# FFN2 of batch 7 by seven block products, a tile of batch 4 as the last piece, and another order of the work

## The chip, the cores and the metric

The kernel runs on one core of a Trainium2 chip. The metric is the time of one execution on the device, in microseconds (us); lower is better. Before the change the median of three runs is 163.83 us (163.65 to 164.19).

The engines, by the names that the profile uses: PE (TensorE) multiplies matrices and writes PSUM, which has eight banks of 128 x 512 fp32; PEld is its loading of weights; DVE (VectorE) and ACT (ScalarE) read PSUM and do elementwise work; POOL (GpSimd) does elementwise work on SBUF and issues the casting loads; SP (SyncE) issues the stores. Each engine takes its instructions in the order in which they were issued to it and waits for the inputs of the next one. 16 DMA engines move the data.

## What is computed

```python
def _attn_ref(q, k, v, phi):                    # 8 batches, 8 heads, 576 rows, D = 64; M = 32
    a = phi - np.max(phi, axis=2, keepdims=True)
    a = np.exp(a)
    a = a / (np.sum(a, axis=2, keepdims=True) + 1e-09)
    k_m = np.einsum('bhsm,bhsd->bhmd', a, k)
    v_m = np.einsum('bhsm,bhsd->bhmd', a, v)
    scores = np.matmul(q, k_m.transpose(0, 1, 3, 2)) / np.sqrt(q.shape[-1])
    scores = scores - np.max(scores, axis=-1, keepdims=True)
    attn = np.exp(scores)
    attn = attn / (np.sum(attn, axis=-1, keepdims=True) + 1e-09)
    return np.matmul(attn, v_m)

def _moe_ref(x, w1, w2, w3, w_out):             # x: 4608 x 512; w1, w2, w3: 512 x 768; w_out: 768 x 512
    h = np.maximum(np.maximum(x @ w1, x @ w2), x @ w3)
    return h @ w_out
```

`x` is the attention's output with the heads side by side. Inputs and output are fp32.

## The kernel before

**What is folded away.** The attention's output of a head is `attn @ v_m`, with only 32 columns in `attn`. So the kernel never forms `x`: for each batch it multiplies `v_m` into the weights (`fold`, line 426) and works on `attn`, whose inner size is 8 heads x 32 = 256. With w1 - w3 and w2 - w3 in place of w1 and w2, the hidden layer is h = max(attn wp_1, attn wp_2, 0) + x w3, and the last part goes straight to the output: out = hT w_out + attn wp3, where wp3 holds v_m, w3 and w_out multiplied together.

**Tiles of rows.** Two batches make a pair with 1152 rows, nine tiles of 128: tiles 0 to 3 of the even batch (rows 0 to 511), tile 4 across both batches (rows 512 to 639), tiles 0 to 3 of the odd batch (rows 640 to 1151).

**The order is written by hand.** The loop at lines 758 to 787 walks a string of words such as `F8@2!` and calls `issue(batch, name, swap)` for each. All engines' instructions come out in that order, and each engine keeps its own share of it. `!` swaps the engine of a step where it has a choice. A second string, `banks` (line 141), gives the PSUM bank of each step that needs one, in the same order; `one_bank` and `two_banks` take the next digit. The names of the steps, with `@b` for the batch:

- L0, L3, L1, L2: loads of phi, q, k, v on POOL's DMA queue (lines 94, 113, 98), 576 KB each. phi and q have two buffers, k and v one for even and one for odd batches.
- r0, r1: pack k and v (L108 on POOL, or L106 on ACT with `!`). E: exponential of phi on ACT (L232).
- B: 72 small matmuls that make k_m and v_m (L250); they need E, r0 and r1. N: normalization on DVE (L270 to L285). K: transposes on PE (L300) and a copy. Q0, Q1: q transposed on DVE (L315). S: scores on PE (L335), then their exponential on ACT (L344).
- a, s, c, m, X: the second normalization, by transpose, sum, reciprocal (DVE), product (POOL, L411) and transpose back (DVE, L419), for two halves 0 and 1.
- D0 to D2: folds of the weights of the hidden layer, D3: fold for wp3 (PE L442, evacuated by ACT or DVE).
- F0 to F11: hidden layer, four matmuls of 288 columns each (L468). An even F ends in a relu on ACT (L173; DVE with `!`, L177), the odd F after it in a maximum on DVE (L481).
- T0 to T4: a plain tile of the output: six matmuls of 512 columns on hT (L658), two on attn (L667; four of half height for T4, L676), a copy by ACT or DVE, a store by SP.

**Seven products.** For the 512 rows of tiles 0 to 3 of a batch, the output can be had from products of blocks half the size: inner size in two halves, output columns in two halves, rows in two groups, seven block products in place of eight, with sums and differences of blocks as operands. Before the change this is done for batches 5 and 6. Its steps:

- U0 to U3 (`combine_w`, line 507): combinations of weight blocks; `U@9` those of w_out, once, 128 x 768 into `tw`; `U@5`, `U@6` those of wp3, 128 x 256. POOL, or DVE with `!`.
- A0 to A3 (`combine_a`, line 552): combinations of blocks of hT, 128 x 768; A4 to A7: of attn, 128 x 256. DVE, or POOL with `!`. A0 and A1 feed one another and then A3; A2 writes over its own block.
- P0 to P6 (`products`, line 565): eight matmuls of 256 columns each (L600). P0, P1 and P2 take a bank each; P3 adds to the bank of P0, P4 to P6 to that of P1. The banks are read into fp32 snapshots (L612 on DVE, L614 on ACT) and added on DVE (L641); two stores of 512 KB follow on SP (L645), the first after P3 and P4, the second after P6.

`combine_w`, `combine_a` and `products` are written for any batch; for batch 7 `sums` (line 521) has buffers of its own, made of those of q, and the output buffers are made of those of phi.

**The last piece.** `ffn2` hands one tile to `ffn2_last` (line 690), which makes it in two column halves of eight matmuls of 256 columns (L699, L707), so that the first half is copied and stored while the second is computed. Before the change this is tile 3 of batch 7.

Of the kernel before, what the change touches and what calls it, by code (L numbers as in the profile page):

```python
# [15 lines left out]
def kernel(  # L16
# [14 lines left out]
    B, H, S, D = q.shape  # L31
# [104 lines left out]
    for i in range(P // M):  # L136
# [4 lines left out]
    banks = iter(  # L141
        "".join(
            """
            00232204420145545045024602460260426042672643424260246024604260462342656204502406
            24062046204267240670462064260246024602064326247420640642064024620462042604605264
            620502645264034063460406064026042640246204203406767676
            """.split()
        )
    )
# [1 line left out]
    def one_bank():  # L151
        return psum[:, int(next(banks))]
# [16 lines left out]
    def evacuate(kind, n, swap, out_, in_, relu=False):  # L169

        if (EVAC[kind][n] == "a") != swap:
            if relu:
                nc.scalar.activation(out=out_, in_=in_, func=AF.Relu)  # L173
            else:
                nc.scalar.copy(out=out_, in_=in_)  # L175
        elif relu:
            nc.vector.tensor_scalar_max(out=out_, in0=in_, scalar1=0.0)  # L177
        else:
            nc.vector.tensor_copy(out=out_, in_=in_)
# [469 lines left out]
    def ffn2(b, t, swap):  # L649


        hT, attn = hts[b // 2], attns[b // 2]
        c0 = S - HP if t == 4 else (b % 2) * (S + HP) + t * P
        if b == B - 1 and t == 3:
            return ffn2_last(b, c0)
        po = one_bank()
        for n, fc in enumerate(fts[b]):
            nc.tensor.matmul(  # L658
                po,
                lhsT=hT[:, fc, c0 : c0 + P],  # L660
                rhs=wo_sb[:, fc, :],
                start=(n == 0),
                stop=False,
            )
        for g in range(NG):
            if t < 4:
                nc.tensor.matmul(  # L667
                    po,
                    lhsT=attn[:, g, c0 : c0 + P],
                    rhs=wp3s[b][:, g, :],  # L670
                    start=False,
                    stop=(g == NG - 1),
                )
            else:
                for u in range(2):
                    nc.tensor.matmul(  # L676
                        po[HP * u : HP * (u + 1)],
                        lhsT=attn[:, g, c0 + HP * u : c0 + HP * (u + 1)],
                        rhs=wp3s[b - 1 + u][:, g, :],
                        start=False,  # L680
                        stop=(g == NG - 1),
                        tile_position=(0, HP * u),
                    )
        ot = opool.tile([P, DM], FP32, name="ot")
        r0 = (b // 2) * 2 * S + c0
        rows = out[r0 : r0 + P, :]
        evacuate("T", t, swap, ot, po)
        nc.sync.dma_start(out=rows, in_=ot)

    def ffn2_last(b, c0):  # L690

        hT, attn = hts[b // 2], attns[b // 2]
        ot = opool.tile([P, DM], FP32, name="ot")
        r0 = (b // 2) * 2 * S + c0
        for i in range(2):
            c = slice(i * DM // 2, (i + 1) * DM // 2)
            po = one_bank()[:, 0 : DM // 2]
            for n, fc in enumerate(fts[b]):
                nc.tensor.matmul(  # L699
                    po,  # L700
                    lhsT=hT[:, fc, c0 : c0 + P],
                    rhs=wo_sb[:, fc, c],
                    start=(n == 0),
                    stop=False,
                )
            for g in range(NG):
                nc.tensor.matmul(  # L707
                    po,
                    lhsT=attn[:, g, c0 : c0 + P],
                    rhs=wp3s[b][:, g, c],  # L710
                    start=False,
                    stop=(g == NG - 1),
                )
            rows = out[r0 : r0 + P, c]
            if i == 0:
                nc.vector.tensor_copy(out=ot[:, c], in_=po)
                nc.sync.dma_start(out=rows, in_=ot[:, c])
            else:
                nc.scalar.copy(out=ot[:, c], in_=po)
                nc.scalar.dma_start(out=rows, in_=ot[:, c])  # L720

    def issue(b, n, swap):
# [22 lines left out]
            "D": lambda: fold(b, i, swap),  # L745
            "F": lambda: ffn1(b, i, swap),
            "T": lambda: ffn2(b, i, swap),
            "U": lambda: combine_w(b, i, swap),
            "A": lambda: combine_a(b, i, not swap),
# [8 lines left out]
    for w in """  # L758
        E@0 H2@0 H0@0 L3@0 Z25@0 B0@0 Y2@0 I@0 N0@0 Z2@0 K0@0! Q0@0 Q1@0 Z9@0 S@0 Z2@0
        M0@0 M1@0 R0@0 R1@0 W0@0 Y3@0 W1@0 W2@0 Z6@0 O1@0 H3@0 O3@0 O2@0 H1@0 X1@0 B1@0  # L760
        X0@0 N1@0 K1@0 O0@0 Y0@0 D1@0! D0@0! D3@0 F8@0 F10@0 F2@0 V0@0 F6@0 F0@0! Y1@0
        D2@0 D4@0 F4@0 L0@1 V1@0 F1@0 E@1 F3@0 L1@1 F5@0 F9@0 F7@0 L3@1 F11@0 B0@1 T3@0
        N0@1 K0@1! L2@1 Q1@1 L2@2 L1@2 Q0@1 L0@2 V2@0 T0@0! L3@2 S@1 T1@0 a0@1 s0@1 c0@1
        m0@1 B1@1 N1@1 a1@1 L1@3 K1@1 s1@1 D0@1 D1@1! D2@1 c1@1 m1@1 X0@1 L3@3 r1@2 X1@1
        T2@0! L2@3 F6@1 F10@1 F7@1 F2@1 F3@1 F4@1 F0@1 r0@2 E@2 F5@1 F1@1 F11@1 L0@3
        L0@4 F8@1 L2@4 F9@1 B@2 D3@1 N@2 Q1@2 T0@1! K@2 T2@1! r0@3 Q0@2 S@2 a0@2 a1@2
        s1@2 c1@2 m1@2 T4@1! D1@2! s0@2 D2@2 c0@2 m0@2 X1@2 D0@2 T3@1 Q0@3 L3@4 X0@2
        Q1@3 T1@1 F0@2 F4@2 F8@2 F6@2 F9@2 E@3 F7@2 F1@2 L1@4 r1@3 F10@2 F2@2 L2@5 B@3
        N@3 D3@2 F3@2 L1@5 F5@2 K@3! U0@9 F11@2 S@3 U1@9 E@4 T3@2 L0@5 T0@2! a1@3 D1@3!
        s1@3 D2@3 a0@3 r1@4 c1@3 L3@5 D0@3 T1@2 m1@3 s0@3 Q0@4 X1@3 c0@3 m0@3 X0@3 T2@2!  # L770
        F4@3! r0@4 F5@3 L2@6 F0@3 D3@3 B@4 F6@3 N@4 F1@3 F8@3 Q1@4 F2@3 F9@3 K@4! F10@3
        r1@5 F7@3 S@4 F11@3 L3@6 D3@4 E@5 r0@5 F3@3 a0@4 U3@9 L0@6 a1@4 T4@3! L1@6 L0@7
        s1@4 D0@4 D1@4! B@5 c1@4 N@5 T1@3 Q1@5 K@5 L1@7 Q0@5 s0@4 c0@4 m0@4 T3@3! S@5
        a0@5 T2@3! s0@5 a1@5 c0@5 X0@4 m1@4 X1@4 D2@4 D0@5 D1@5 m0@5 s1@5 X0@5 T0@3!
        F4@4 c1@5 F2@4 m1@5 r1@6 L2@7 F10@4 r0@6 F3@4 F5@4 F8@4 X1@5 F9@4 F0@4 F11@4
        F6@4 E@6 F10@5! F7@4 L3@7 F0@5 F2@5 A4@5! Q0@6 A5@5! F1@4 F1@5 A7@5! F8@5 F6@5
        F4@5! Q1@6 D3@5 B@6 N@6 r0@7 D2@5 T0@4! F7@5 F5@5 K@6 F3@5 U2@9 F9@5 U0@5! T1@4!
        F11@5 A0@5 A6@5 r1@7! E@7 S@6 T2@4! D1@6! U1@5! D2@6 a0@6 Q1@7 B@7 A1@5! U2@5
        U3@5 N@7 T3@4 s0@6 K@7! Q0@7 a1@6 P1@5 D3@6 s1@6 c1@6 S@7 c0@6 A2@5! m1@6 P2@5
        P4@5 a0@7 s0@7 D3@7 D2@7 m0@6 a1@7 c0@7 D1@7! P0@5! A3@5! U0@6 s1@7 P5@5 c1@7  # L780
        m1@7 X1@6 X0@6 T4@5! D0@6! D0@7 P6@5 U1@6 m0@7 F8@6 F9@6 F6@6 U3@6 U2@6 X0@7
        P3@5 F10@6 F2@6 X1@7 F11@6 F8@7 F0@6 F3@6 F7@6 F4@7 F1@6 F9@7 F4@6 A4@6 F5@6
        F2@7 F0@7 F5@7 A0@6! A6@6! A1@6! F6@7 F10@7! F3@7 A5@6! P1@6 A2@6! F1@7 P0@6
        F7@7 A3@6! F11@7 P2@6! P4@6 T0@7 T1@7 P5@6! A7@6 T4@7 P6@6! P3@6! T2@7! T3@7
    """.split():
        n, b = w.rstrip("!").split("@")
        issue(int(b), n, w.endswith("!"))
# [30 lines left out]
```

## Time and profile before

| | |
|---|---|
| runs, median (lowest, highest) | 163.83 us (163.65, 164.19) |
| the profiled execution's own time | 164.42 us |
| its span, first to last instruction | 162.4 us |
| PE busy | 152.6 us (94%) |
| DVE busy | 104.5 us (64%) |
| ACT busy | 97.8 us (60%) |
| POOL busy | 92.2 us (57%) |
| matmuls of FFN1 (L468) | 384, 50.2 us |
| matmuls of plain tiles (L658) | 162, 39.6 us |
| granted TensorE clock | 0.998 |
| DMA | 31.76 MB, mean 196 GB/s |

A line of the timeline or of the groups gives start and length in us, engine, line, operation, output and input by their names in the program, and shapes as partitions x elements. Matmuls are pipelined: the length of one is longer than the distance from one to the next, so the cost of a matmul is read from how far apart groups begin, or from the chain. The chain of waits goes back from the last instruction, at each step to what released it; between two entries of the same engine nothing was waited for.

### The profile page before, as it was taken

Reading aid. Unit: us, or ns where it says so; the run is one execution under the profiler, and the core shown is the slowest. Engines: PE = TensorE matmul, PEld = TensorE weight load, DVE = VectorE, ACT = ScalarE, POOL = GpSimd, SP = SyncE. Lnnn points to the kernel's source line nnn. Section 1 sums busy time; section 2 is a strip of 40 time slices with the busy share of each in tenths; the row PEclk is TensorE's granted clock in tenths of the full one; section 3 lists DMA queues with packets and bytes.
Section 4 is the critical chain, followed back from the end, with each engine's and each line's share of the span. In section 5 each row is a group of like instructions: output and inputs, shape, how many; then the busy total and the mean of one; then the engine's idle time right before and its main releaser. Section 6 shows DMA issues by size and latency. Waiting matters only on the chain.

```text
span 162.4 us, 4946 instructions
## 1 busy us (share of the span) xinstructions
PE 152.6 (94%) x2128; PEld 90.5 (56%) x2128; DVE 104.5 (64%) x201; ACT 97.8 (60%) x144; POOL 92.2 (57%) x92
## 2 busy tenths in 40 slices
PE   7958798999798999999999999999999999999991
PEld 2433544673366535753584536776456577785570
DVE  2013703898837847577487797986999967874340
ACT  4204535934497468977689849688779786631110
POOL 7931115100598359899877964999094880395000
PEclk9999999999999999999999999999999999999999
DMA  5999999999999999999999999999221044000365
GB/s 153 152 205 208 206 211 214 276 208 210 250 323 232 212 244 378 261 237 205 261 318 230 212 312 306 286 183 174 84 96 65 4 164 160 4 0 0 129 253 199
DMA packets 21909, 31.76 MB, mean 196 GB/s; under 512 B 1152, under 2 KB 16512, under 8 KB 21888
## 3 DMA queue, kind: packets, MB, share of 16 engines
q0 software_dynamic: 16080, 21.43, 69.1%
q1 hardware_dynamic: 5664, 9.90, 17.3%
q8 instruction: 16, 0.26, 0.6%
q10 hardware_dynamic: 144, 0.13, 0.2%
q14 instruction: 5, 0.04, 0.1%
HBM read 39.32 MB, written 9.44 MB: 300 GB/s over the span
## 4 chain that ended last, share of the span: by engine, by line
PE 62%; DMA 27%; DVE 4%; POOL 3%; ACT 1%; issue 1%; POOLq 0%
PE psum L468 22%; PE psum L658 17%; DMA ph<-in_phi_dram 15%; DMA w_sb<-in_moe_w_dram 12%; PE psum L600 8%; PE psum L667 5%; PE psum L442 4%; PE psum L250 2%; POOL kvo L98 2%; PE psum L676 1%; PE psum L335 1%; DVE twb L505 1%; PE psum L699 1%; ACT e L232 1%; PE psum L300 1%
## 5 line engine op out<-in xcount | busy, mean ns | idle before, releaser
L468 PE MATMUL psum<-attn,wp 128*128 128x288 bf16 x384 | 50.2, 286 | 0.2
L468 PEld LDWEIGHTS <-wp 128*128 128x128 bf16 x384 | 36.9, 98 | 12.0 <-issue 1.5
L481 DVE TENSOR_TENSOR hT<-psum,h 128x576 bf16<-128x576 f32 x48 | 34.5, 752 | 12.7 <-PE psum L468 8.3
L658 PE MATMUL psum<-wo_sb,hT 128*128 128x512 bf16 x162 | 39.6, 380 | 0.0
L173 ACT ACTIVATE h<-psum 128x576 bf16<-128x576 f32 x43 | 26.1, 657 | 7.2 <-PE psum L468 7.1
L175 ACT CAST wp<-psum 128x1024 bf16<-128x1024 f32 (+1 forms) x30 | 28.4, 996 | 2.6 <-PE psum L442 2.6
L175 ACT COPY ot<-psum 128x512 f32<-128x512 f32 x23 | 13.6, 591 | 23.2 <-PE psum L667 18.2
L411 POOL TENSOR_TENSOR t<-t,sm 128x576 bf16<-128x576 bf16 x14 | 16.1, 1154 | 19.2 <-DVE sm L406 19.2
L108 POOL COPY kvr<-kvo 128x2304 bf16<-128x2304 bf16 x11 | 23.2, 2111 | 5.5 <-DMA kvo<-in_k_dram 4.4
L658 PEld LDWEIGHTS <-hT 128*128 128x128 bf16 x162 | 14.6, 98 | 17.8 <-issue 3.2
L667 PE MATMUL psum<-wp,attn 128*128 128x512 bf16 x46 | 13.7, 379 | 0.0
L344 ACT ACTIVATE e<-psum 128x576 bf16<-128x576 f32 x16 | 9.6, 653 | 6.1 <-PE psum L335 6.1
L162 PE MATMUL psum<-warm 128*128 128x512 bf16 x44 | 12.1, 428 | 1.2 <-DVE warm L131 1.2
L315 DVE STREAM_TRANSPOSE qT<-qq 128x576 f32<-128x576 f32 x16 | 12.0, 760 | 1.1 <-DMA qq<-in_q_dram 1.0
L232 ACT ACTIVATE e<-ph 128x1152 bf16<-128x1152 f32 (+1 forms) x9 | 9.5, 1061 | 2.9 <-DMA ph<-in_phi_dram 2.7
L98 POOL DMA_DIRECT2D kvo<-in_v_dram x9 | 6.8, 753 | 7.4 <-PE psum L250 4.1
L397 DVE TENSOR_REDUCE sm<-t 128x18 f32<-128x576 bf16 x14 | 10.4, 740 | 0.2
L113 POOL DMA_DIRECT2D qq<-in_q_dram x8 | 6.1, 759 | 6.3 <-DMA w_sb<-in_moe_w_dram 6.0
L250 PEld LDWEIGHTS <-e 64*32 64x32 bf16 x720 | 7.1, 90 | 4.5 <-issue 2.8
L389 DVE STREAM_TRANSPOSE t<-e 128x288 f32<-128x288 f32 x14 | 6.5, 468 | 4.0 <-ACT e L344 4.0
L98 POOL DMA_DIRECT2D kvo<-in_k_dram x9 | 6.9, 769 | 2.9 <-DMA qq<-in_q_dram 2.1
L419 DVE STREAM_TRANSPOSE attn<-t 128x288 f32<-128x288 f32 x14 | 6.2, 456 | 3.5 <-POOL t L411 3.5
(94 smaller groups left out, 181.0 us busy)
## 6 DMA issues: line engine op xcount, KB each, us to landing
out_dram<-ot SPq DMA_DIRECT2D x27, 256.0 KB, 6.0
qq<-in_q_dram POOLq DMA_DIRECT2D x8, 576.0 KB, 14.0
ph<-in_phi_dram POOLq DMA_DIRECT2D x7, 576.0 KB, 16.0
kvo<-in_k_dram POOLq DMA_DIRECT2D x7, 576.0 KB, 15.9
kvo<-in_v_dram POOLq DMA_DIRECT2D x7, 576.0 KB, 16.7
w_sb<-in_moe_w_dram POOLq DMA_DIRECT2D x3, 768.0 KB, 19.4
out_dram<-oj SPq DMA_DIRECT2D x4, 512.0 KB, 2.8
wo_sb<-in_moe_w_out_dram POOLq DMA_DIRECT2D x1, 768.0 KB, 15.0
```

Of the source, the lines that this page charges most:

```text
L98: nc.gpsimd.dma_start(out=kv[:, i, h].rearrange("p j c d -> p j (c d)"), in_=by_pair((k, v)[i], b)[:, h],)
L108: nc.gpsimd.tensor_copy(out=out_, in_=in_)
L162: nc.tensor.matmul(po[:, 0:BANK], lhsT=warm[:, 0:P], rhs=warm, start=True, stop=True)
L173: nc.scalar.activation(out=out_, in_=in_, func=AF.Relu)
L175: nc.scalar.copy(out=out_, in_=in_)
L315: nc.vector.transpose(out=s["qT"][:, j].rearrange("p j c r e -> p (j c r e)").bitcast(FP32), in_=loaded[b]["q"][:, j].rearrange("p j c d - ...
L411: (nc.vector if swap else nc.gpsimd).tensor_tensor(out=t, in0=t, in1=s["sm", g].unsqueeze(2).to_broadcast([P, S // HP, R, 2]), op=ALU.mult,)
L468: nc.tensor.matmul(acc[:, h, 0:SH], lhsT=wps[b][:, g, w * DF + ft * P : w * DF + (ft + 1) * P], rhs=attn[:, g, c0 : c0 + SH], start=(g == ...
L481: nc.vector.tensor_tensor(out=hT[:, ft, (b % 2) * S : (b % 2 + 1) * S].rearrange("p (h n) -> p h n", h=2), in0=a, in1=s["h1", ft], op=ALU.max,
L600: nc.tensor.matmul(po[:, q * CH : (q + 1) * CH], lhsT=lhs(k, q), rhs=rhs(k), start=(i < 3 and k == 0 and q == 0), stop=(k == KT and q == 1 ...
L658: nc.tensor.matmul(po, lhsT=hT[:, fc, c0 : c0 + P], rhs=wo_sb[:, fc, :], start=(n == 0), stop=False,)
L667: nc.tensor.matmul(po, lhsT=attn[:, g, c0 : c0 + P], rhs=wp3s[b][:, g, :], start=False, stop=(g == NG - 1),)
```

## The change

`T0@7` to `T3@7` leave the string; `U0@7` to `U3@7`, `A0@7` to `A7@7` and `P0@7` to `P6@7` come in. `ffn2` now hands tile 3 of batch 4, `T3@4`, to `ffn2_last`, and that word moves from the middle of the work to the end. The order is another from `F9@1` on, with new banks from that point and `!` set or taken at some 38 steps. All other code stays.

```diff
@@ -141,9 +141,9 @@
     banks = iter(
...
@@ -651,7 +651,7 @@
 
         hT, attn = hts[b // 2], attns[b // 2]
         c0 = S - HP if t == 4 else (b % 2) * (S + HP) + t * P
-        if b == B - 1 and t == 3:
+        if (b, t) == (4, 3):
             return ffn2_last(b, c0)
         po = one_bank()
         for n, fc in enumerate(fts[b]):
@@ -763,25 +763,26 @@
         N0@1 K0@1! L2@1 Q1@1 L2@2 L1@2 Q0@1 L0@2 V2@0 T0@0! L3@2 S@1 T1@0 a0@1 s0@1 c0@1
         m0@1 B1@1 N1@1 a1@1 L1@3 K1@1 s1@1 D0@1 D1@1! D2@1 c1@1 m1@1 X0@1 L3@3 r1@2 X1@1
         T2@0! L2@3 F6@1 F10@1 F7@1 F2@1 F3@1 F4@1 F0@1 r0@2 E@2 F5@1 F1@1 F11@1 L0@3
-        L0@4 F8@1 L2@4 F9@1 B@2 D3@1 N@2 Q1@2 T0@1! K@2 T2@1! r0@3 Q0@2 S@2 a0@2 a1@2
-        s1@2 c1@2 m1@2 T4@1! D1@2! s0@2 D2@2 c0@2 m0@2 X1@2 D0@2 T3@1 Q0@3 L3@4 X0@2
-        Q1@3 T1@1 F0@2 F4@2 F8@2 F6@2 F9@2 E@3 F7@2 F1@2 L1@4 r1@3 F10@2 F2@2 L2@5 B@3
-        N@3 D3@2 F3@2 L1@5 F5@2 K@3! U0@9 F11@2 S@3 U1@9 E@4 T3@2 L0@5 T0@2! a1@3 D1@3!
-        s1@3 D2@3 a0@3 r1@4 c1@3 L3@5 D0@3 T1@2 m1@3 s0@3 Q0@4 X1@3 c0@3 m0@3 X0@3 T2@2!
-        F4@3! r0@4 F5@3 L2@6 F0@3 D3@3 B@4 F6@3 N@4 F1@3 F8@3 Q1@4 F2@3 F9@3 K@4! F10@3
-        r1@5 F7@3 S@4 F11@3 L3@6 D3@4 E@5 r0@5 F3@3 a0@4 U3@9 L0@6 a1@4 T4@3! L1@6 L0@7
-        s1@4 D0@4 D1@4! B@5 c1@4 N@5 T1@3 Q1@5 K@5 L1@7 Q0@5 s0@4 c0@4 m0@4 T3@3! S@5
-        a0@5 T2@3! s0@5 a1@5 c0@5 X0@4 m1@4 X1@4 D2@4 D0@5 D1@5 m0@5 s1@5 X0@5 T0@3!
-        F4@4 c1@5 F2@4 m1@5 r1@6 L2@7 F10@4 r0@6 F3@4 F5@4 F8@4 X1@5 F9@4 F0@4 F11@4
-        F6@4 E@6 F10@5! F7@4 L3@7 F0@5 F2@5 A4@5! Q0@6 A5@5! F1@4 F1@5 A7@5! F8@5 F6@5
-        F4@5! Q1@6 D3@5 B@6 N@6 r0@7 D2@5 T0@4! F7@5 F5@5 K@6 F3@5 U2@9 F9@5 U0@5! T1@4!
-        F11@5 A0@5 A6@5 r1@7! E@7 S@6 T2@4! D1@6! U1@5! D2@6 a0@6 Q1@7 B@7 A1@5! U2@5
-        U3@5 N@7 T3@4 s0@6 K@7! Q0@7 a1@6 P1@5 D3@6 s1@6 c1@6 S@7 c0@6 A2@5! m1@6 P2@5
-        P4@5 a0@7 s0@7 D3@7 D2@7 m0@6 a1@7 c0@7 D1@7! P0@5! A3@5! U0@6 s1@7 P5@5 c1@7
-        m1@7 X1@6 X0@6 T4@5! D0@6! D0@7 P6@5 U1@6 m0@7 F8@6 F9@6 F6@6 U3@6 U2@6 X0@7
-        P3@5 F10@6 F2@6 X1@7 F11@6 F8@7 F0@6 F3@6 F7@6 F4@7 F1@6 F9@7 F4@6 A4@6 F5@6
-        F2@7 F0@7 F5@7 A0@6! A6@6! A1@6! F6@7 F10@7! F3@7 A5@6! P1@6 A2@6! F1@7 P0@6
-        F7@7 A3@6! F11@7 P2@6! P4@6 T0@7 T1@7 P5@6! A7@6 T4@7 P6@6! P3@6! T2@7! T3@7
+        F8@1 L2@4 F9@1 D3@1 B@2 N@2 Q1@2 U0@9 Q0@2 T1@1! K@2 T0@1! S@2 a0@2 r0@3 s0@2
+        c0@2 a1@2 D0@2 s1@2 L1@4 Q0@3 c1@2 Q1@3 T2@1 L0@4 D3@2 m0@2 D1@2! m1@2 D2@2 L3@4
+        T3@1 T4@1! E@3 r1@3 X0@2 X1@2 F6@2! F0@2! L1@5 F4@2 F1@2 F8@2 B@3 F10@2 N@3 F9@2
+        U1@9 F7@2 K@3! F5@2 F2@2 S@3 L2@5 F11@2 F3@2 a1@3 D2@3 D0@3 T3@2 E@4 a0@3 s0@3
+        U3@9 L0@5 c0@3 s1@3 c1@3 r1@4 r0@4 T0@2 D3@3 D1@3! B@4 m0@3 m1@3 N@4 X0@3 X1@3
+        T2@2 Q1@4 K@4! Q0@4 F6@3 F8@3! F10@3 F0@3 F7@3 L3@5 F4@3 F9@3 S@4 F1@3 r0@5 F2@3
+        a1@4 F5@3 L2@6 a0@4 D3@4 s1@4 D1@4! F3@3 F11@3 E@5 T1@2 D0@4 r1@5 s0@4 c1@4 D2@4
+        B@5 L0@6 c0@4 m1@4 N@5 T3@3 Q1@5 Q0@5 K@5! L1@6 T2@3! S@5 L2@7 T4@3! a0@5 D0@5
+        s0@5 c0@5 a1@5 m0@4 D1@5! X0@4 X1@4 D2@5! r1@6 L1@7 L3@6 m0@5 T1@3 F0@4 s1@5
+        X0@5 c1@5 F4@4 F10@4 F5@4 m1@5 r0@6 U2@9 F1@4 X1@5 F6@4 F8@4 F7@4 L0@7 E@6 F11@4
+        F2@5 F2@4! r1@7 F3@5 A4@5! F9@4 F4@5 F0@5 F3@4 D3@5 U0@5 B@6 F10@5 N@6 F8@5 L3@7
+        A6@5! F5@5 F6@5 F1@5 r0@7! F11@5 K@6 F9@5 F7@5 E@7 T0@3! Q0@6 Q1@6 D3@6 D0@6 B@7
+        U2@5 A0@5! T1@4 N@7 Q1@7 U1@5 S@6 U3@5 Q0@7 A1@5! a1@6 s1@6 c1@6 K@7! T4@5 S@7
+        A5@5! A2@5! m1@6 a1@7 A3@5! a0@6 T2@4! D2@6 s1@7 a0@7 c1@7 s0@6 s0@7 X1@6 D0@7
+        m1@7 D1@6! T0@4! c0@6 P1@5! c0@7 D1@7! m0@6 m0@7 D3@7 D2@7! X0@6 P2@5! P4@5
+        P0@5! F2@6 F10@6 X1@7 X0@7 P5@5 A7@5! U0@7 F3@6 F0@6 A4@6! P3@5! P6@5 F1@6 F8@6
+        U1@7 F9@6 F8@7 F2@7 F11@6 F3@7 F4@6 F5@6 A4@7! F10@7 F9@7 F6@6 U2@6 F0@7! F11@7
+        F4@7 F5@7 U0@6 F7@6 F1@7 P1@6 A0@6 A5@7! F6@7 A1@6 A3@6 F7@7 A0@7 U1@6 A5@6!
+        P2@6 A2@6 A7@7 U3@7 P0@6 U3@6 A7@6! P1@7 A1@7 P2@7! P4@6 P3@6! P4@7 A6@7! U2@7!
+        A6@6! A2@7 A3@7 P5@6! P0@7! P5@7! P6@6 P3@7 P6@7! T4@7 T3@4
     """.split():
         n, b = w.rstrip("!").split("@")
         issue(int(b), n, w.endswith("!"))
```

More of the change, by code (lines that the diff above doesn't have):

```diff
@@ L143 @@
             """
-            00232204420145545045024602460260426042672643424260246024604260462342656204502406
-            24062046204267240670462064260246024602064326247420640642064024620462042604605264
-            620502645264034063460406064026042640246204203406767676
+            00232204420145545045024602460260426042672643424260246024604260426726403406202604
+            26024062046204674026720624602460246024026542463640260264026042604264026420624030
+            46246302616240124604626224064260420624602640250125014
             """.split()
```

## The prediction

> **What bounds the kernel now.** I read the page's first two parts, then the chain of waits in order of time, then the timelines of PE, ACT and POOL, then the landing time of each load, one DMA issue at a time.
>
> The page: how busy each engine is, then PE and DMA in 40 slices of 4.06 us.
>
> ```profile
> span 162.4 us, 4946 instructions
> ...
> PE 152.6 (94%) x2128; PEld 90.5 (56%) x2128; DVE 104.5 (64%) x201; ACT 97.8 (60%) x144; POOL 92.2 (57%) x92
> ...
> PE   7958798999798999999999999999999999999991
> ...
> DMA  5999999999999999999999999999221044000365
> ```
>
> Two things are full: PE from slice 14 on, and the DMA engines until slice 28, which is about 114 us. The end of the span follows PE, but the loads run just ahead of it for two thirds of the time.
>
> The chain (start us, us, what) shows the last point at which a load held PE, and the size of the pieces that matter later.
>
> ```profile
> 27.17 24.16 DMA ph<-in_phi_dram
> 51.34 0.02 issue
> 51.36 1.17 ACT e L232
> 52.53 0.04 issue
> 52.58 0.80 PE psum L250 x69
> ...
> 126.13 1.85 PE psum L600 x16
> ...
> 148.79 0.43 PE psum L667 x2
> 149.22 1.29 PE psum L658 x6
> ...
> 157.25 0.66 PE psum L699 x6
> 157.90 0.22 PE psum L707 x2
> 158.12 0.66 PE psum L699 x6
> 158.77 0.23 PE psum L707 x2
> ```
>
> phi of batch 2 lands (51.34), ACT takes its exponential (E@2, 1.17 us), PE starts B@2 at 52.58. From there to 159.01 the windows give PE 106.29 us busy in 106.44: 0.15 us idle. So after 52.58 a change gains only what it takes off PE, and loses whatever it makes PE wait.
>
> The timelines of ACT and PE around the next such point, and the DMA issue of L0@3 (made at 51.24; the last figure is us to landing):
>
> ```profile
> 64.62 2.28 ACT L173 ACTIVATE h<-psum 128x576 bf16<-128x576 f32 x4
> 66.97 1.16 ACT L232 ACTIVATE e<-ph 128x1152 bf16<-128x1152 f32 x1
> ```
>
> ```profile
> 63.93 4.57 PE L468 MATMUL psum<-attn,wp 128*128 128x288 bf16 x36
> 68.43 0.80 PE L250 MATMUL psum<-kvr,e 64*32 64x129 bf16 x72
> ```
>
> ```profile
> ph<-in_phi_dram POOLq DMA_DIRECT2D x1, 576.0 KB, 15.7
> ```
>
> phi of batch 3 lands at 51.24 + 15.7 = 66.94; E@3 starts at 66.97, ends at 68.13; B@3 starts at 68.43, after nine FFN1 blocks of batch 2 (0.50 us each: 63.93 to 68.43). The old order reaches B@3 0.25 us after it can start. That slack decides this change.
>
> **The change, part by part.**
>
> *Work taken off PE.* Out: T0, T1, T2 of batch 7, plain, 1.29 + 0.43 = 1.72 each, T3@7 in halves, 0.66 + 0.22 + 0.66 + 0.23 = 1.77, and T3@4 plain, 1.72: together 8.65. In: seven products of eight 256-column matmuls; two take 1.75 to 1.85 in the chain, mostly 0.87 each, so 6.09, and T3@4 in halves, 1.77: 7.86. Net **-0.79 us**. The 56 weight loads (98 ns each) lie under matmuls that follow one another every 0.87 / 8 = 109 ns, as in batches 5 and 6; without that cover seven products would cost 56 x 98 ns = 5.5 us more.
>
> *D3@1 goes ahead of B@2.* PE idles 0.52 us before B@2, and D3@1 takes 0.23, with its inputs long there: **-0.23** (0 if its banks are late). The 0.15 idle, a wait of S@3 at 71.05, need not recur: -0.15 to 0; I take -0.15.
>
> *B@3 goes ahead of four FFN1 blocks.* Between B@2 and the first F@2 the new order has the same PE work as the old (five tiles T, K, S, folds; D3@2 in place of D3@1), so F@2 starts again at 63.93. Then five blocks, not nine, stand ahead of B@3: PE is there at 63.93 + 5 x 0.50 = 66.43. Its inputs: L0@3 and everything queued for load before it are issued as before, until 51.24, and loads land in the order of issue, so L0@3 lands at 66.94, E@3 ends at 68.13, B@3 starts at 68.18. PE waits 68.18 - 66.43 = **+1.75**. V of batch 3 says nearly the same: L2@3 lands at 65.15, and POOL's pack r1@3 (65.17, 2.10 us) ends at 67.27. Queued behind: on ACT the relus of F4@2 and F8@2 stand behind E@3 and free the banks of F10@2 and F9@2; at 0.6 us each after 68.1 they are done (68.7, 69.3) as PE gets there (68.8, 69.3), so no second wait. All of PE's later work shifts.
>
> Sum so far: -0.79 - 0.23 - 0.15 + 1.75 = **+0.58**.
>
> *Loads and packs after that.* L0@4 goes behind L2@4, U0@9 (POOL 1.67), r0@3 (2.11) and L1@4; U1@9 and U3@9 move among the packs; L2@7 goes ahead of L1@7, L3@6 and L0@7; r0@7 goes from POOL to ACT. There is always a load still waiting when the next is issued, so the DMA engines keep their pace, and I lay the old landings, 1.6 to 4.3 us apart, on the new order. B@4: L1@4 lands near 74, POOL's r1@4, r0@4 run to 77.1, L0@4 lands near 76, E@4 ends at 77.1; PE comes at 77.6. B@5: L0@5 keeps its place (88.5), E@5 ends at 89.65, PE comes at 89.5: +0.15. B@7, some 4 us earlier than before: L0@7 lands near 111.6, behind L3@6; E@7 ends at 114.2 behind r0@7 on ACT; PE comes at 114.4. I take **+0.15** for all; the bounds are 0 and +1.4 (each landing is off by up to one old spacing between neighbours of the same kind, about 1.2).
>
> *New combinations and evacuations.* Batch 7 gets eight A and four U. DVE: A0 to A3 at 0.56, A7 and U2 at 0.28; POOL: three A, three U at 0.67. Batch 6's A0 to A3 go from POOL (1.64) to DVE (0.56); U0, U1, A0 and A6 of batch 5 go the other way, while PE is still in other work. Four evacuations become seven (0.59 on ACT, 0.69 on DVE). DVE was busy 6.88 of 15.12 us from 143.9 on; ten combinations (about 5 us) and three more adds or copies (2 us) make some 14 of 16. Laid out by hand, DVE lags PE by about 1.5 us but delivers A0, A1, A3 of batch 6 and A1, A2, A3 of batch 7 0.5 to 1 us before their products. Earlier, at 118 to 129 us, DVE is as full (X0@6 ends 0.4 before F2@6). Cost **+0.1**, bounds 0 and +1.0.
>
> How DVE and POOL share: at 117.84 DVE's 128x256 combination took 1.75 us, where the same form took 0.28 at 115.41; POOL's 1.64 us combination had begun at 117.81, and DVE's ended 0.14 after it. The Trainium skill says so under "SBUF: two separate sides" (SBUF — State Buffer): a DVE instruction with two SBUF inputs and a GpSimd one that reads SBUF lock each other out for a whole instruction. The trace agrees, with that 1.75. What it would do here is the third rival.
>
> *The tail.* P3@7, P6@7, T4@7, then T3@4 in halves give PE the finish it had (P3@6, T2@7, T3@7). Their stores are 512 + 512 + 256 + 128 + 128 KB, and P6@6's 512 KB now falls 1 us ahead of them. The old burst ran at 350 to 400 GB/s and drained by 160.15; 512 KB more is 1.4 us at that rate, most of it in the empty time before 155. From PE's end to the span's end was 162.4 - 159.0 = 3.4. **+0.05**, bounds 0 and +0.6.
>
> Total: 0.58 + 0.15 + 0.1 + 0.05 = **+0.9 us**. The profiled execution took 164.42 for a span of 162.4, so 2.0 lie around the span; it is 0.59 above the median of the three runs, 163.83. Against the median: 163.83 + 0.88 = **164.7 us**.
>
> **Rivals.**
>
> 1. *Faster: B@3 is not held so long.* What matters is when B@3 starts: the sum changes sign if it starts before 68.18 - 0.88 = 67.3. If phi alone came earlier, r1@3 would still hold it until 67.3: 163.83 + 0.88 - 0.88 = 163.8; if V too were 0.9 earlier, PE would not wait: 163.83 - 1.17 = 162.7, with the small terms 163.0. For: L0@4 no longer follows directly behind L0@3, and several loads are in flight at a time (some 16 us from issue to landing, 1.6 to 4.3 from one landing to the next). Against: what is queued ahead of L0@3 is untouched, and ACT's E@3 began 0.03 after the landing. Chance 0.18, times 162.7 to 163.8.
>
> 2. *Later loads hold PE as well.* E@4, E@5 and E@7 stand in ACT's queue ahead of evacuations, so a late phi also keeps banks. With landings 1.2 late at one of them: 164.7 + 1.2 = 165.9. For: the three come within 0.5 us of PE by my layout. Against: PE late at B@3 gives all of them that time. Chance 0.22.
>
> 3. *DVE and POOL lock each other out in the tail.* The combinations that POOL has in its last stretch are 0.67 each; if eight met ten of DVE's, DVE would wait up to 8 x 0.67 = 5.4 us and PE for what exceeds DVE's slack, some 2 us: 166.7. Against: POOL's inputs (attn, wp3) are early, its 15 of 0.67 from about 128 end near 140, before A0@6 can start at 143.8. Chance 0.04.
>
> **How the numbers follow.** Forecast 0.54, on its own 164.2 to 165.4; the rivals 0.18, 0.22, 0.04; 0.02 is left. A change of 0.3% (0.49 us, 163.34 to 164.32) is about what a measurement of this kernel can tell from none. Of the forecast 0.45 lies above 164.32, 0.09 within; of rival 1, 0.13 below and 0.05 within; rivals 2 and 3 lie above. Faster 0.13, same 0.16, slower 0.71. The range runs from rival 1's end to just short of rival 3: 162.7 to 166.4.
>
> **What would show it.** Of step one: seven products at 0.87, PE busy 0.8 less after B@2. Of the hold: PE idle of 1.5 to 2 us before B@3's L250 near 66.4 to 68.2, released by ACT e L232, with L0@3 landing near 66.9; the chain should run back through that phi load, not the one of batch 2. Of the loads: idle under 0.3 before B@4, B@5, B@7. Of the tail: DVE's L505 at 0.28 and 0.56, none at 1 us or more, and 3.4 to 3.6 us from PE's end to the span's. I am wrong if B@3 starts before 67.3, or if PE waits over 1 us anywhere else.

## The result, and the profile after

| | median | runs | ratio to before, 95% interval |
|---|---|---|---|
| before | 163.81 us (163.01 to 164.72) | 20 | |
| changed | 164.31 us (163.65 to 165.46) | 20 | 1.0035 (1.0018 to 1.0051) |

The changed kernel is 0.5 us slower. A second series, on another occasion, gave 164.03 to 163.77, 1.0025 (1.000 to 1.005). The forecast was +0.88 and 164.7.

The first two profiled executions can't be set against each other directly. The one before took 164.42, which is 0.6 above its median; the one of the changed kernel took 163.67, which is 0.6 below its own. They say "0.75 faster" where forty runs say "0.5 slower". So each kernel was profiled once more, and that pair lies near the medians: 163.93 before, 164.38 changed.

| execution | time | span | L0@3 lands | PE's wait at B@3 | PE ends | PE's end to span's end | last store, issue to landing |
|---|---|---|---|---|---|---|---|
| before, first | 164.42 | 162.4 | 66.94 | 0 | 159.01 | 3.4 | 1.8 |
| before, again | 163.93 | 162.0 | 65.6 | 0 | 158.60 | 3.4 | 1.8 |
| changed, first | 163.67 | 161.8 | 64.66 | 0 | 157.57 | 4.2 | 2.8 |
| changed, again | 164.38 | 162.5 | 65.38 | 0.38 | 157.74 | 4.7 | 3.3 |

The page of the changed kernel (first execution): span, the busy times, and PE and DMA in 40 slices of 4.05 us.

```profile
span 161.8 us, 5014 instructions
...
PE 151.5 (94%) x2152; PEld 92.7 (57%) x2152; DVE 109.8 (68%) x212; ACT 96.0 (59%) x140; POOL 94.4 (58%) x100
...
PE   7958798999799999999999999999999999999990
...
DMA  5999999999999999999999999999222124000394
```

PE is as full as before and busy 1.1 us less; DVE is busy 5 us more. The last four digits of DMA, 0394, show the stores pushed together at the end, where before they were 0365.

The chain of waits of the changed kernel, in order of time, around B@3 and at the end:

```profile
63.77 2.56 PE psum L468 x20
66.33 0.73 PE psum L250 x70
...
142.50 11.35 PE psum L600 x104
153.86 1.29 PE psum L658 x6
...
157.34 0.23 PE psum L707 x2
157.57 0.02 issue
157.59 0.37 ACT ot L719
```

PE comes to B@3 at 66.33 after five FFN1 blocks, and the chain goes on through PE: no phi load stands in it. At 142.50 thirteen products follow one another, 11.35 / 13 = 0.873 us each. The timeline of ACT in the same execution shows why there was no hold:

```profile
64.68 1.17 ACT L232 ACTIVATE e<-ph 128x1152 bf16<-128x1152 f32 x1 [0.28 <-DMA ph<-in_phi_dram]
```

ACT was waiting for phi of batch 3, as forecast, but phi had come by 64.66, 2.3 us earlier than in the first profile of before. In the second execution of the changed kernel the hold is there, much smaller. Its chain, and PE's timeline at that place:

```profile
51.10 14.28 DMA ph<-in_phi_dram
65.38 0.02 issue
65.40 1.17 ACT e L232
66.58 0.04 issue
66.62 0.80 PE psum L250 x68
```

```profile
66.62 0.80 PE L250 MATMUL psum<-kvr,e 64*32 64x129 bf16 x72 [0.38 <-ACT e L232]
```

The order of events is that of the forecast (phi, E@3, B@3), and the bracket, which is PE's idle time just before B@3, gives its price: 0.38 us, not 1.75.

What is left is the end. The DMA view from 151 to 164 us, 40 slices of 0.325 us, before (again) and after that the changed kernel (first execution); under each, stores with their size and the median time from issue to landing (`ox` and `oj` are the two stores of the products, `ot` those of plain tiles):

```profile
DMA  3008930000019909999999999995600000000000
...
out_dram<-oj SPq DMA_DIRECT2D x2, 512.0 KB, 3.1
...
out_dram<-ot ACTq DMA_DIRECT2D x1, 128.0 KB, 1.8
```

```profile
DMA  0000000279999999999999999500000000000000
GB/s 0 0 0 0 0 0 0 50 302 365 321 378 372 378 334 397 397 384 397 384 366 384 375 337 315 196 25 22 22 0 0 0 0 0 0 0 0 0 0 0
...
q8 instruction: 1, 0.02, 0.7%
...
out_dram<-ox SPq DMA_DIRECT2D x2, 512.0 KB, 4.7
out_dram<-oj SPq DMA_DIRECT2D x1, 512.0 KB, 4.2
out_dram<-ot SPq DMA_DIRECT2D x1, 256.0 KB, 3.6
out_dram<-ot SPq DMA_DIRECT2D x1, 128.0 KB, 3.2
out_dram<-ot ACTq DMA_DIRECT2D x1, 128.0 KB, 2.8
```

In the changed kernel nothing moves from 151 to 153.3; then the DMA engines are full without a gap until 159, for 3 x 512, 256 and 2 x 128 KB. After that three slices (0.9 us) carry 22 to 25 GB/s, a sixteenth of the 390 before them: one of 16 engines is still at work. From 159.42 to 160.42 the trace has 22 packets, one after another, and they fill 6.4% of the 16 engines' time, which is 1.02 of one engine. The second execution has four such slices (1.3 us), the one of before none. The last 128 KB lands 2.8 us after its issue (3.3 in the second execution), against 1.8.

This last store ends in 16 small packets, and they show that the burst as a whole hardly delays the end. Fifteen of them were through 1.85 us after PE's end (2.10 in the second execution), against 1.82 in the near-median execution of before. The sixteenth came 1.01 us after those (1.30), against 0.02 before.

The `q8 instruction` line above is a packet of 16 KB that the kernel before does not have at that place. The pages count such packets over the whole execution, before and then changed:

```profile
q8 instruction: 16, 0.26, 0.6%
q8 instruction: 17, 0.28, 0.6%
```

The one in the burst ran from 153.44 to 154.85 (153.88 to 155.58 in the second execution); in the kernel before the last one had ended by 142.8. With nothing else moving, at about 141 to 147, such a packet took 0.93 to 1.46 us in the profiles. The records don't say which engine took it; that it was the engine that came last is an inference, taken up again below.

PE ended 0.86 us sooner than in the near-median execution of before (157.74 against 158.60), and the end of the span came 1.33 us later behind it (4.74 against 3.41): together +0.47, which is the +0.5 of the medians.

### The profile page after: what moved, and what is told of

It reads as the page before. It is cut to its first block, busy times and chain, and to the rows that moved or that the text cites. A ratio compares the mean times of both kernels' runs of the same rounds, so it can differ in the third digit from the quotient of the medians.

```text
span 161.8 us, 5014 instructions
## 1 busy us (share of the span) xinstructions
PE 151.5 (94%) x2152; PEld 92.7 (57%) x2152; DVE 109.8 (68%) x212; ACT 96.0 (59%) x140; POOL 94.4 (58%) x100
## 4 chain that ended last, share of the span: by engine, by line
PE 82%; DMA 9%; DVE 2%; POOL 2%; issue 1%; ACT 1%; DVEq 0%; POOLq 0%
PE psum L468 29%; PE psum L658 19%; PE psum L600 11%; DMA wo_sb<-in_moe_w_out_dram 9%; PE psum L667 5%; PE psum L442 5%; PE psum L250 4%; PE psum L195 3%; PE psum L335 2%; PE psum L676 1%; DVE hT L481 1%; PE psum L699 1%; PE psum L300 1%; POOL kvo L98 1%; DVE h L177 0%
## 5 line engine op out<-in xcount | busy, mean ns | idle before, releaser
L481 DVE TENSOR_TENSOR hT<-psum,h 128x576 bf16<-128x576 f32 x48 | 34.5, 752 | 8.4 <-PE psum L468 5.0
L658 PE MATMUL psum<-wo_sb,hT 128*128 128x512 bf16 x138 | 33.7, 380 | 0.0
L173 ACT ACTIVATE h<-psum 128x576 bf16<-128x576 f32 x42 | 25.9, 657 | 9.5 <-PE psum L468 9.5
L658 PEld LDWEIGHTS <-hT 128*128 128x128 bf16 x138 | 12.2, 98 | 14.9 <-issue 2.9
L175 ACT COPY ot<-psum 128x512 f32<-128x512 f32 x17 | 10.1, 592 | 13.2 <-PE psum L667 10.9
L315 DVE STREAM_TRANSPOSE qT<-qq 128x576 f32<-128x576 f32 x16 | 11.5, 752 | 1.2 <-DMA qq<-in_q_dram 1.0
L344 ACT ACTIVATE e<-psum 128x576 bf16<-128x576 f32 x16 | 9.6, 653 | 3.5 <-PE psum L335 3.5
L667 PE MATMUL psum<-wp,attn 128*128 128x512 bf16 x38 | 11.3, 379 | 0.0
L270 DVE RECIPROCAL rden<-psum 128x2 f32<-128x2 f32 x8 | 1.4, 169 | 10.7 <-PE psum L250 10.7
```

The lines of the kernel that those rows point to most:

```text
L481: nc.vector.tensor_tensor(out=hT[:, ft, (b % 2) * S : (b % 2 + 1) * S].rearrange("p (h n) -> p h n", h=2), in0=a, in1=s["h1", ft], op=ALU.max,
L658: nc.tensor.matmul(po, lhsT=hT[:, fc, c0 : c0 + P], rhs=wo_sb[:, fc, :], start=(n == 0), stop=False,)
L667: nc.tensor.matmul(po, lhsT=attn[:, g, c0 : c0 + P], rhs=wp3s[b][:, g, :], start=False, stop=(g == NG - 1),)
```

## The experiments

Two theories were at stake. The one on record: the hold at B@3 sets the result, and the tail costs next to nothing. The rival, formed on the two profiles: the hold is small, since phi is usually early, and the burst of stores at the end costs about a microsecond. In the experiments every time is a median, and every ratio is to runs of the kernel before on the same chip; the whole reference is computed in all of them. The cuts from the order string are joined to one line each, and the banks that go with them are left out.

**Both kernels once more.** No edit.

> The changed kernel once more, unedited, for a second profile. In the first one phi of batch 3 landed at 64.66, 2.3 us earlier than in the profile of before, B@3 was not held, PE ended at 157.57, and the span went on for 4.23 us after it (before: 3.39). Theory A (the loads' pace differs from one execution to the next; where it is that of the profile of before, B@3 is held): if this execution is at the median (164.3) or above, phi of batch 3 lands at 66 or later and PE idles 0.8 us or more before B@3. Theory B (the stores at the end cost 0.8 us in every execution, and loads play no part): no idle before B@3 whatever the time, and 4.1 to 4.4 us from PE's end to the span's end. Both can hold.

> The kernel before once more, unedited, for a second profile of it. Theory A: its landing of phi of batch 3 lies anywhere from 64.5 to 67.5; if early, PE starts B@2 and B@3 as soon as its order lets it and the time is 163.0 to 163.5, which is below the 164.42 of the first profile by about what the landing is earlier than 66.9. Theory B: from PE's end to the span's end 3.3 to 3.5 us. Against the kernel before: a ratio of 1.000 within its interval.

Changed 164.03, 1.0025 (1.000 to 1.005); before against itself 1.0000 (0.9978 to 1.0022). The rows are in the table above: the tail of the changed kernel is long in both of its executions, and the hold is 0 in one and 0.38 in the other.

**Stores by halves.** Each product stores its 256 KB as soon as they are summed, in place of two stores of 512 KB after n = 4 and n = 6; once in the changed kernel, and once in the kernel before as a control.

```diff
-            if n in (4, 6):
-                r0 = b * S + (b % 2) * HP
-                rows = out[r0 : r0 + 2 * TW].rearrange("(q r p) c -> p q r c", q=2, r=2)
-                nc.sync.dma_start(out=rows[:, :, n // 5], in_=acc["ot"][n // 5])
+            r0 = b * S + (b % 2) * HP
+            rows = out[r0 : r0 + 2 * TW].rearrange("(q r p) c -> p q r c", q=2, r=2)
+            cols = slice(0, CH) if n in (2, 6) else slice(CH, DM)
+            nc.sync.dma_start(out=rows[:, :, n // 5, cols], in_=ot)
```

> The changed kernel, but each 256-column half of a product's output is stored as soon as it is there (P2, P4 with P3, P5, P6: four stores of 256 KB per batch in place of two of 512 KB), so that of the last two batches some 1 MB and not 1.8 MB is left for the last 5 us. Theory B (the end waits for the stores): from PE's end to the span's end 3.4 to 3.6 us in place of 4.23, and the time 0.6 to 0.8 us below the changed kernel, at about 163.6. Rival (that time is spent on something else than the amount of data, such as the last store's own latency): still 4.1 to 4.3 us, time as the changed kernel. If rows of 1 KB move slower than rows of 2 KB, the gain is smaller, 0 to 0.5.

> The kernel before, with the stores of its products (batches 5 and 6) by column halves as in the earlier run. Theory B (the gain of 0.7 to 1.0 us that halves gave the changed kernel is the store burst that the seventh batch of products put into the last 5 us): here the burst is 1 MB smaller and drained in time, so the gain is small: 0 to 0.25 us, and from PE's end to the span's end 3.2 to 3.4 us (3.39 before). Rival (smaller stores help wherever they stand, whatever the burst): 0.6 us or more gained here too.

In the changed kernel 163.30, 0.9971 (0.9951 to 0.9992): 0.73 below the changed kernel of the same series. In the kernel before 163.83, 0.9994 (0.9974 to 1.0014): nothing. The DMA view of the changed kernel with halves, same window:

```profile
DMA  0079600399993992099409985091000000000000
...
out_dram<-ox SPq DMA_DIRECT2D x3, 256.0 KB, 3.3
...
out_dram<-ot ACTq DMA_DIRECT2D x1, 128.0 KB, 1.7
```

The first stores are now done at 152.6, there are gaps between them, the last store is back at 1.7, and from PE's end to the span's end it is 3.7. The same edit gains nothing where there was no such burst, so it is the burst that it cures. From PE's end to the span's end the control too has 3.7, 0.3 more than without halves, though its last store lands after 1.7; why was not tried. This is the only version here that lies clearly under the kernel before.

**B@3 later.** E@3 and B@3 go back behind four more FFN1 blocks, which takes the possible hold away.

```diff
-T3@1 T4@1! E@3 r1@3 X0@2 X1@2 F6@2! F0@2! L1@5 F4@2 F1@2 F8@2 B@3 F10@2 N@3 F9@2 U1@9 F7@2 K@3! F5@2 F2@2 S@3 L2@5 F11@2 F3@2 a1@3
+T3@1 T4@1! r1@3 X0@2 X1@2 F6@2! F0@2! L1@5 F4@2 F1@2 F8@2 F10@2 E@3 F9@2 U1@9 F7@2 F5@2 B@3 N@3 F2@2 F11@2 K@3! F3@2 S@3 L2@5 a1@3
```

> The changed kernel, but E@3 and B@3 stand four FFN1 blocks of batch 2 later (after F10, F9, F7, F5), where the order before had B@3; K@3, S@3 and two folds move with them, and F11 comes ahead of S@3. Theory A (held at B@3 in part of the executions, by up to 1.75 us): median 0.3 to 0.9 below the changed kernel, and its slowest executions lose most. Rival (no hold in the timed executions, or one that later loads put back at B@5 and B@7): median within 0.2 of the changed kernel. From PE's end to the span's end 4.1 to 4.4 as in the changed kernel.

165.54, 1.0107 (1.0076 to 1.0137): slower than the changed kernel. PE's timeline:

```profile
67.08 1.63 PE L468 MATMUL psum<-attn,wp 128*128 128x288 bf16 x12 [0.25 <-ACT h L173]
...
70.90 0.28 PE L300 MATMUL psum<-ident,kvn 128*128 128x128 bf16 x2 [0.28 <-DVE kvn L285]
...
73.03 0.41 PE L442 MATMUL psum<-w_sb,kvt 64*32 64x512 bf16 x8 [0.45 <-ACT e L344]
```

phi had landed at 64.79 in this execution, so there was no hold to take away. In its place come three waits, 0.98 together: a relu on ACT (L173), N@3 on DVE (L285) and the exponential after S@3 on ACT (L344) each have too little PE work between them and what needs them. The edit mixes the loss of the hold with the loss of these covers; it shows only that the hold is not what the changed kernel usually pays.

**P6@6 earlier.** The first 512 KB of the burst are moved ahead, with the stores uncut: first behind A6@6, A2@7, A3@7 and P5@6, then (second version) with P4@7 between P5@6 and P6@6. Each also with halves (in the second for batch 7 alone).

```diff
-P4@6 P3@6! P4@7 A6@7! U2@7! A6@6! A2@7 A3@7 P5@6! P0@7! P5@7! P6@6 P3@7 P6@7! T4@7 T3@4
+P4@6 P3@6! A6@7! U2@7! A6@6! A2@7 A3@7 P5@6! P6@6 P4@7 P0@7! P5@7! P3@7 P6@7! T4@7 T3@4
```

```diff
-P4@6 P3@6! P4@7 A6@7! U2@7! A6@6! A2@7 A3@7 P5@6! P0@7! P5@7! P6@6 P3@7 P6@7! T4@7 T3@4
+P4@6 P3@6! A6@6! P5@6! P4@7 A6@7! U2@7! A2@7 A3@7 P6@6 P0@7! P5@7! P3@7 P6@7! T4@7 T3@4
```

> The changed kernel with one thing moved: P5@6 and P6@6 come right after P3@6 (with the combinations that they need), ahead of P4@7, P0@7, P5@7, so that the last 512 KB of batch 6 are stored some 2.6 us earlier, where the DMA engines are idle; no store is cut. Theory B: the last stores are 512 + 512 + 256 + 128 + 128 KB as in the kernel before, and from PE's end to the span's end it is 3.4 to 3.7 us in place of 4.2 to 4.8; the last store lands in 1.8 to 2.2 us; time 0.6 to 1.0 below the changed kernel, 163.2 to 163.5. Rival (the two 512 KB stores of batch 7 alone keep the queue full): 4.0 or more, gain under 0.4. If DVE is late with A2@7 and A3@7 in the new place, PE waits before P5@7 or P3@7.

> Both: P5@6 and P6@6 early, and stores by halves. Theory B: from PE's end to the span's end 3.3 to 3.5 us, 0.2 to 0.4 under halves alone (3.7), at about 163.0 to 163.2, which is 0.4% below before. Rival: nothing over either one alone.

> The changed kernel with P5@6 and P6@6 early once more, now with P4@7 between the two (in the first try PE stood 1.71 us before P6@6, which adds to the bank that DVE's addition after P5@6 still had to read, behind A2@7 and A3@7 in DVE's queue), and that addition ahead of U2@7, A2@7, A3@7. Theory B (the end waits for a store burst): no wait of PE among the products, PE ends at 157.6 to 157.9, 3.4 to 3.7 us follow it, the last store lands in 1.8 to 2.2 us; time 163.2 to 163.6, which is 0.6 to 1.0 below the changed kernel. Rival (the gain of halves was not the burst): 164.0 to 164.3.

> The same, and batch 7's products stored by halves (four of 256 KB in place of two of 512), those of batches 5 and 6 not. Theory B: the last store lands in 1.7 to 1.8 us, and 3.3 to 3.6 us follow PE's end; time 163.0 to 163.4, 0 to 0.3 below early P6 alone, since most of the burst is already gone.

First version: 165.43, 1.0090 (1.0062 to 1.0117), with halves 165.57, 1.0091 (1.0062 to 1.0120). DVE's and PE's timelines in it:

```profile
148.93 0.55 DVE L505 TENSOR_TENSOR sx<-hT,sx 128x768 bf16<-128x768 bf16 x1
149.40 0.68 DVE L641 TENSOR_TENSOR oj<-psum,ln 128x512 f32<-128x512 f32 x1
```

```profile
150.14 0.81 PE L600 MATMUL psum<-w3T,hT 128*128 128x256 bf16 x6 [1.71 <-DVE oj L641]
```

P6@6 adds to the bank that DVE's addition after P5@6 must first read, and DVE had A2@7 and A3@7 ahead of that addition: a wait of the edit's own making. Second version: 163.65, 0.9983 (0.9957 to 1.0008), with halves 163.79, 0.9993 (0.9965 to 1.0020); the last store lands after 2.0 and 1.8 us, and from PE's end to the span's it is 3.8 and 3.4. So the tail also shortens when the stores stay whole and only one of them leaves the burst. Even the spoiled first version had a last store of 2.0 and a tail of 3.7. The times missed what was expected: both forms of the first version by about 2 us, mostly through that wait, the second by 0.05 and its form with halves by 0.4, for halves gained nothing more there.

**The old order in front, the new end behind.** The order of before up to the folds of batch 7, then the changed kernel's steps from F2@6 on. T3@4 is missing from the front in both, since it is the last piece. In the second version T4@5 stands in T3@4's old place, and P6@5 and P3@5 are back near their old places.

```diff
-U3@5 N@7 s0@6 K@7! Q0@7 a1@6 P1@5 ... X1@6 X0@6 T4@5! D0@6! D0@7 m0@7 F2@6 F10@6 X1@7 X0@7 U0@7 F3@6 F0@6 A4@6! P3@5! P6@5 F1@6
+U3@5 N@7 T4@5! s0@6 K@7! Q0@7 a1@6 P1@5 ... X1@6 X0@6 D0@6! D0@7 P6@5 m0@7 P3@5 F2@6 F10@6 X1@7 X0@7 U0@7 F3@6 F0@6 A4@6! F1@6
```

> The order of before up to the fold D0@7 (its loads, packs and B steps where they stood), and from there the changed kernel's end: products of batch 7, T3@4 last, the same combinations, stores as in the changed kernel; new banks for that part. Theory B: PE's work is 0.8 less, so PE ends 0.7 to 0.9 before the 158.60 of the second profile of before, at about 157.8, and 4.2 to 4.8 us follow it: time 0.2 to 0.5 us above before, as the changed kernel. So the new order of the front is worth nothing either way. Theory A (the new front is held by loads in part of the executions, 0.38 us in the last profile): old_front is 0.2 to 0.4 us faster than the changed kernel, at the time of before or just under it.

> The order of before for loads, packs, B steps and batches up to 5, with the changed kernel's end, once more; in the first try PE waited 1.42 us for N@7 at K@7, since T3@4 had covered that, and 1.21 us for the cast of D0@6 at F2@6. Now T4@5 stands where T3@4 stood, and P6@5, P3@5 come between D0@6 and F2@6. If the covers hold: PE ends at 157.6 to 158.0 (158.60 in the second profile of before, less 0.79), 4.2 to 4.8 us follow, time 163.9 to 164.4, the same as the changed kernel: the seven products and the place of T3@4 make all of the change, and the rest of the new order nothing. If the new order gains by itself, this is slower than the changed kernel by 0.3 or more without a wait over 0.3 us; if the changed kernel's hold at B@3 costs in most executions, this is faster by 0.2 to 0.4.

First: 167.78, 1.0235 (1.0199 to 1.0270). Second: 164.90, 1.0074 (1.0050 to 1.0097). PE's timeline of the first, then of the second:

```profile
121.55 0.23 PE L300 MATMUL psum<-ident,kvn 128*128 128x128 bf16 x1 [1.42 <-DVE kvn L274]
...
132.06 2.13 PE L468 MATMUL psum<-attn,wp 128*128 128x288 bf16 x16 [1.21 <-DVE wp L179]
```

```profile
128.11 0.63 PE L442 MATMUL psum<-w_sb,kvt 64*32 64x512 bf16 x16 [0.80 <-ACT wp L175]
```

T3@4's 1.72 us of matmuls had covered DVE's normalization N@7; without them PE waits 1.42 there. In the second version that wait is gone, and one of 0.80 is left at a fold whose bank ACT empties late. PE ends at 158.41 and the tail is 4.7. The time is 0.5 above the range in which it would have been that of the changed kernel. Taking the 0.80 off gives a span of 162.3, beside 161.8 and 162.5 of the changed kernel: by this, what the new order in front does is fill T3@4's place, and it gains or loses nothing that shows here. That the wait could be had for nothing was not tried, so this stays an inference.

**A later phi.** L0@3 and L2@4 change places in POOL's queue.

```diff
-L0@3 F8@1 L2@4
+L2@4 F8@1 L0@3
```

> The changed kernel with the loads L0@3 (phi of batch 3) and L2@4 (v of batch 4) in each other's place, 0.74 us apart on POOL's queue. It measures what a hold at B@3 costs. Theory A (loads land in the order of issue, a phi that lands late holds E@3 and B@3, and PE never gets that time back): L0@3 lands 2.5 to 4 us later, at 67.5 to 69; B@3 starts 1.2 us after it; PE waits there for what that exceeds 66.3, 2.4 to 3.9 us, and the time goes up by 0.7 to 1.0 of the wait, 1.8 to 3.9 us. Rival (loads issued together share the engines, so the order of two neighbours hardly matters): L0@3 lands within 1 us of where it did, wait under 1.

169.08 from four runs (166.8, 168.73, 169.42 and 169.5); the ratio, 1.0233 (1.0159 to 1.0307), is that of the two lower ones. The wait was expected at 2.4 to 3.9, the loss at 1.8 to 3.9: the wait came out so, the loss is larger. PE at B@3, and the windows of the profiled execution (start:end, length; busy us and instructions of PE, PEld, DVE, ACT, POOL; then the granted clock, the DMA share and GB/s):

```profile
69.39 1.18 PE L250 MATMUL psum<-kvr,e 64*32 64x129 bf16 x72 [3.20 <-ACT e L232]
```

```profile
60.00:66.00 6.00, 6.00 (x38) 3.19 (x37) 4.87 (x10) 3.52 (x5) 5.47 (x5) 1.00 1.16 277
66.00:69.39 3.39, 0.20 (x2) 0.00 (x0) 0.63 (x1) 1.21 (x2) 3.36 (x4) 0.85 1.11 293
69.39:71.00 1.61, 1.60 (x75) 1.23 (x76) 0.32 (x2) 1.03 (x2) 1.61 (x3) 0.50 1.12 322
71.00:73.00 2.00, 2.00 (x10) 1.30 (x9) 0.94 (x4) 0.65 (x1) 2.00 (x2) 0.50 1.14 319
73.00:75.00 2.00, 2.00 (x12) 1.38 (x11) 1.34 (x3) 0.48 (x1) 2.00 (x2) 0.50 1.19 211
75.00:77.00 2.00, 2.00 (x46) 1.06 (x45) 0.96 (x2) 1.41 (x3) 0.07 (x1) 0.96 1.21 208
```

phi lands at 68.2, 2.8 later than in the second execution of the changed kernel, and PE's wait grows by the same 2.8, from 0.38 to 3.20: the chain phi, E@3, B@3 is what sets B@3, microsecond for microsecond, once phi is late. PE's end moves further, by 5.35 (163.09 against 157.74). The other 2.5 us are in the granted clock: it is 0.50 while PE works from 69.39 to about 75.2, so 5.8 us of PE time did half their work, some 2.9 us lost by this estimate.

## Why it came out so, point by point

**Work off PE (-0.79): right.** From the start of B@2 to PE's end it is 106.55 us in the near-median execution of before (52.05 to 158.60) and 105.61 in that of the changed kernel (52.13 to 157.74), -0.94, of which D3@1's move out of that stretch is -0.23. In between, the windows give these busy times of PE, first before, then changed (same columns as above):

```profile
52.60:157.50 104.90, 104.60 (x1401) 64.29 (x1386) 77.61 (x148) 70.29 (x101) 68.58 (x59) 1.00 0.76 184
```

```profile
52.60:157.50 104.90, 104.33 (x1432) 67.42 (x1417) 83.27 (x160) 68.02 (x97) 70.57 (x66) 1.00 0.78 185
```

The idle time is 0.30 and 0.57, so the work in the stretch fell by 0.94 + 0.27 = 1.21, against 0.79 + 0.23 = 1.02 by the sum, 0.19 more than forecast. The products take 0.87 each, and their weight loads stay hidden.

**D3@1 into the idle time before B@2 (-0.23), and the 0.15 idle (-0.15): half right.** In the near-median execution of before PE doesn't wait for phi of batch 2 at all; B@2 starts at 52.05 and not at 52.58. With D3@1 ahead of it, B@2 starts 0.08 later, so the move was worth 0.15. The old idle did not come back, but one of 0.19 at 70.75, where a maximum of DVE (L481) is late, took its place.

**The hold at B@3 (+1.75): the mechanism right, the size wrong.** By its own sign ("I am wrong if B@3 starts before 67.3") the prediction failed here: B@3 started at 66.26 and 66.62. PE was forecast at B@3 at 66.43 and came at 66.24 in the second execution. phi was forecast at 66.94; in the twelve later profiles with the same queue ahead of it, it landed at 64.4 to 65.8. L0@2 shows that this is not the change's doing: issued at the same point in every kernel, it landed at 51.34 in the first profile of before and at 49.4 to 50.7 in all others. The step that failed is "L0@3 lands at 66.94": it was read from one execution, and that one's loads were among the latest. The time of that execution, 0.59 above its median, was in the text as an offset of the whole, and not as a warning about its loads. Measured: 0 to 0.38. The experiment with the later phi shows the mechanism at full size; there the sum would also have needed the half clock.

**Later loads (+0.15) and DVE (+0.1): right in size.** No wait at B@4, B@5 or B@7 in the changed kernel; the one of DVE is the 0.19 above. Rival 2 did not occur: in the changed kernel no load held PE by more than 0.38. Rival 3 did not either: DVE's combinations (L505) took 0.28 to 0.56 in both executions. With the old order in front the 1.75 us of the first profile came back, at 118.31, so the lock is there with the old order, and the new one doesn't meet it.

**The tail (+0.05): wrong, and this is what makes the kernel slower.** The step was "512 KB more is 1.4 us at that rate, most of it in the empty time before 155". The rate was right, but the step reckoned with the mean rate of all engines to the last byte. In the first execution the stores of P6@6, P3@7 and P6@7 are issued within 2.5 us from 152.8 on, the engines then have no gap for 5.5 us, and the last 0.9 us (1.3 in the second) go at a sixteenth of the rate. Measured: +0.8 and +1.3 at the end, beyond the bound of 0.6 and nearly the length of those last stretches. Fifteen engines kept within the forecast's bound (1.85 and 2.10 us after PE's end, against 1.82), one did not. Halves take back 0.73 of the time, an earlier P6@6 brings the ratio to before from 1.0025 and 1.0035 down to 0.9983, and the control shows no gain where the slow stretch was absent.

Why one engine is late is an inference from all fourteen profiles. In the six that have the 16 KB `instruction` packet and the whole burst (the changed kernel twice, the later B@3, both old fronts, the later phi), the last of the 16 closing packets came 0.95 to 1.49 us after the fifteenth. In the five that have the packet in a burst opened by halves or by the earlier P6@6 it came 0.02 to 0.23 after it, and in the three of the old order, which have no such packet in their last 8 us, 0.02 to 0.03. It looks as if the engine that takes this packet falls about a microsecond behind and, in a burst without gaps, can't make it up. The burst without the packet was not tried.

So the sum, +0.88, is near the +0.5 of the runs by luck, through two errors that cancel: the hold 1.4 to 1.75 too large, the tail 0.7 to 1.3 too small. Rival 1, for which B@3 is not held, was the true course of the front; its time of 163.0 would have come out with the old tail (164.38 - 1.33 = 163.05). The halves, which come nearest to that, have 163.30.

## What to carry to other kernels

A hold behind a queued load is priced from several executions: here the same load, with the same queue ahead of it, landed anywhere within 2.5 us, and the one profile at hand, 0.6 above the median, had it latest of all. Work moved to the end moves its stores there: count the bytes issued in the last 5 us against the drain rate of the trace, leave gaps in which a late engine can catch up, see whether an `instruction` packet falls among them, and store each part as soon as it is summed. A step taken out of the middle is also a cover taken away; look at what stood behind it (T3@4: 1.42 us).

## What the runs showed of the hardware

The end of a burst isn't at the rate of the burst: after 5.5 us at up to 397 GB/s the last 0.9 us (1.3 in the second execution) went at 22 to 28 GB/s, the rate of one engine in 16, while the other fifteen were done. A 16 KB packet of the `instruction` queue took 1.41 and 1.70 us in the burst, and 0.93 to 1.46 with nothing else moving. That it is what makes the one engine late is inferred, not tried.

An idle PE costs more than its idle time. In the wait of 3.20 us, after a last matmul that ended at 66.19, the granted clock is 0.85 over 66.00 to 69.39: 1.0 us of that stretch was at 0.50, so the clock fell at about 68.4, 2.2 us after that matmul. It was back at about 75.2 (0.96 over 75 to 77), 5.8 us after PE had started again. After waits of 1.71 and 1.42 us in other kernels it stayed at 1.00. The Trainium skill says under "Part 1: The HAM clock gate" (TensorE: Matmul & The Clock Gate) that a window of about 3.4 us without work halves the clock, and that about as long a stretch of work brings it back. The trace agrees with the halving, but it came after 2.2 us without work, and the way back took longer, 5.8 us. The four runs from 166.8 to 169.5 suggest that the half clock doesn't last equally long in all of them. Their mean granted clocks go from 0.995 (166.8) down to 0.979 (169.5), but a whole profile is there only of the last, and runs of the changed kernel itself have 0.984 to 1.000, so this stays open.
